# Chunk 1's second layer by seven products, with the sums for it spread over GpSimd and VectorE

## The chip, the core and the metric

The kernel runs on one core of a Trainium2 chip. The metric is the time of one execution in device microseconds. TensorE (PE, its weight loads PEld) multiplies into PSUM; VectorE (DVE), ScalarE (ACT) and GpSimd (POOL) work on what lies in SBUF or, GpSimd excepted here, in PSUM; SyncE (SP) and GpSimd issue the transfers. Each engine works off its own instructions strictly in the program's order.

## The reference

Strided sparse attention, and then a layer pair with a leaky kink between the layers. All inputs and the output are float32.

```python
# q, k, v: (8, 8, 576, 64); stride 32; heads 0-3 local, heads 4-7 strided
scores = np.matmul(q, k.transpose(0, 1, 3, 2)) / np.sqrt(64)
mask_local   = (rel >= 0) & (rel < 32)          # rel = query position - key position
mask_strided = (rel >= 0) & (key % 32 == query % 32)
attn = softmax(where(mask, scores, -1e9))
x = matmul(attn, v) -> (4608, 512)
h = x @ w_in                                    # (512, 2048)
g = np.maximum(h, 0.0) + alpha * np.minimum(h, 0.0)
out = g @ w_out                                 # (2048, 512)
```

## The kernel before

The 4608 tokens are nine chunks of 512. For a chunk the first layer makes gT, 2048 features by 512 tokens in fp16, in 16 pieces (`lin1_piece`: four matmuls of 512 columns into a PSUM bank, Relu of the negative by ScalarE, the sum by VectorE, which writes one sixteenth of gT). The second layer multiplies gT with w_out.

Between these pieces TensorE does the attention of the next batch. It is cut into steps that stand in one list, `pieces`, and `attn_step` takes the next one: S are the scores of a pair of heads (`score_both`: matmuls, exponentials by ScalarE, then a multiplication with the mask), P a product with v (`pv_piece`, with a reciprocal and a multiplication by VectorE), T a turn of q or k (`transpose_piece`), X a turn of the result into xT, which is what the first layer reads. Some results are turned by a transfer instead (`x_dma`, and `x_copy` by ScalarE after it). A pair g belongs to batch g // 4; its heads are local for g % 4 below 2, strided above. The second half of an S's exponentials and its mask are put off to the next steps (`defer`). The steps also issue casts and loads for later batches.

The main loop runs over the chunks n from 1 and over i: i below 16 are pieces of the first layer, i from 16 are parts of the second. After each, a share of the attention steps is dealt out by an accumulator (`acc`). Chunk 0 stands in a list written out by hand before that loop, with the second layer of chunk 0 (`U`, `W`) and the attention of batch 1.

There are two forms of the second layer. `lin2_piece`, which chunk 1 takes, has 16 parts of four matmuls of 512 columns. `lin2_fast`, which chunks 2 to 8 take, computes the same by seven products in place of eight: gT is split in halves by token and by even and odd features, w_out in halves by column and by even and odd features, and the products are made of sums and differences of the quarters. It has 14 parts of eight matmuls of 256 columns. It needs four tiles of differences of w_out (`wsum`, made once, by `wout_sum` during chunk 1's second layer, each one VectorE operation of 128 x 2048) and four tiles of sums of gT (`gsum`, made for every chunk, each in two halves of 128 x 1024 by `g_sum`; two of the eight halves go to GpSimd, six to VectorE). Its parts stand in the order of products 1, 5, 6, 2, 7, 3, 4, two parts each. Product 5 reads gsum0 and wsum0, product 6 gsum1 and wsum1, product 7 gsum2 and wsum2, product 3 gsum3, product 4 wsum3. Products 3 and 7 end in a store that adds a saved part by VectorE (L688).

The mask multiplications are at L396 (VectorE, for pairs of batch 1), L401 and L408 (GpSimd, for all later pairs). `hps` and `ops` banks come from a PSUM pool of three, the banks of S's second half, P, T and X from another pool of three ("ps").

Of the kernel before, what the change touches and what calls it, by code (L numbers as in the profile page):

```python
# [9 lines left out]
F32 = mybir.dt.float32  # L10
# [22 lines left out]
def kernel(  # L33
# [50 lines left out]
    DX = 2  # L84
# [271 lines left out]
    def score_both(P, eng=None):  # L356

        w, r = P.w, 72 if P.strided else 128
        for i in range(2):
            et = ets[ectr["i"] % NE]  # L360
            ectr["i"] += 1
# [26 lines left out]
            if eng is not None:  # L388
                if i == 0:
                    keep(nc.scalar.activation(  # L390
                        ev.rearrange("r (y c) -> r y c", y=2), sp[0:r, :, 0:n], AF.Exp, scale=SCALE))
# [4 lines left out]
                keep(nc.vector.tensor_tensor(mv, mv, m, op=ALU.mult))  # L396
                continue
            if i == 0:
                keep(nc.scalar.activation(  # L399
                    ev.rearrange("r (y c) -> r y c", y=2), sp[0:r, :, 0:n], AF.Exp, scale=SCALE))  # L400
                keep(nc.gpsimd.tensor_tensor(mv, mv, m, op=ALU.mult))  # L401
                continue

            def ex(y):
                keep(nc.scalar.activation(  # L405
                    ev[:, n * y : n * y + n], sps[y][0:r, 0:n], AF.Exp, scale=SCALE))
                if y:
                    keep(nc.gpsimd.tensor_tensor(mv, mv, m, op=ALU.mult))  # L408

            defer_et["et"] = et  # L410
            defer.extend([lambda: ex(0), lambda: ex(1)])
# [88 lines left out]
    for g in range(7, npair + 2):  # L500
# [30 lines left out]
        for i, (kind, fn) in enumerate(seq):  # L531
# [6 lines left out]
            def run(fn=fn, extra=extra, g=g, c=c, kind=kind, lastp=(i == lastP), first=(i == 0),  # L538
                    second=(i == min(1, len(seq) - 1))):
                fn()  # L540
                for b, pr in extra:
                    if pr in ("q", "k"):
                        if b < NX:
                            cast_l(b, pr)
                        if b + 1 < NX:
                            load_qk(b + 1, pr)
                        continue
                    cast_v(b, pr, "pool")
                    if pr == 1 and b + 1 < B:
                        load_v(b + 1, True)  # L550
# [4 lines left out]
                if lastp:  # L555
                    if 4 * DX <= g - 1 < npair and pairs[g - 1].xd:
                        x_dma(pairs[g - 1])
                    if g % 4 == 3 and DX < c + 1 < B:
                        transpose_d()
                    if g % 4 == 2 and DX <= c and c + 1 < B:  # L560
                        load_d(c + 1)
                    if g % 4 == 1 and DX <= c and c + 1 < B:
                        load_v(c + 1, False)
                    if g % 4 == 1 and NX <= c + 2 < B:
                        load_rows(c + 2, "q")
                    if g == 8:
                        load_v(3, True)
# [54 lines left out]

    ops_cur = {}

    def lin2_piece(n, i):
        mt, part = i // 4, i % 4
        last = n == NCH - 1
        if part == 0:
            ops_cur["t"] = phpool.tile([128, 512], F32, tag="hps", name="ops")
        ops = ops_cur["t"]  # L630
        r0 = 512 * n + 128 * mt
        if last and mt == 3:

            if part in (1, 3):
                return
            c0 = 128 * part
            half = phpool.tile([128, 512], F32, tag="hps", name="ops3") if part else ops
            for kf in range(16):
                keep(nc.tensor.matmul(
                    half[:, 0:256], gTs[n][:, kf, 128 * mt : 128 * mt + 128],  # L640
                    wout16[:, kf, c0 : c0 + 256], start=(kf == 0), stop=(kf == 15)))
            osb = opool.tile([128, 512], F32, tag="osb", name="osb")
            keep(nc.vector.tensor_copy(osb[:, 0:256], half[:, 0:256]))
            keep(nc.sync.dma_start(out[r0 : r0 + 128, c0 : c0 + 256], osb[:, 0:256]))
            return
        for kf in range(4 * part, 4 * part + 4):
            keep(nc.tensor.matmul(  # L647
                ops, gTs[n][:, kf, 128 * mt : 128 * mt + 128], wout16[:, kf, :],
                start=(kf == 0), stop=(kf == 15)))
        if part == 3:  # L650
            osb = opool.tile([128, 512], F32, tag="osb", name="osb")
            keep(nc.scalar.copy(osb, ops))
            keep(nc.sync.dma_start(out[r0 : r0 + 128, :], osb))


    def wout_sum(i):

        def w(j, c):
            return wout16.rearrange("p (i j) c -> p i j c", j=2)[:, :, j, 256 * c : 256 * c + 256]

        o, a, b = (
            (0, w(0, 1), w(0, 0)), (1, w(1, 1), wsum[0]),
            (2, w(1, 1), w(0, 1)), (3, w(1, 0), wsum[1]))[i]
        keep(nc.vector.tensor_tensor(wsum[o], a, b, op=ALU.subtract))

    def g_sum(n, i, h, eng="dve"):

# [260 lines left out]
                keep(nc.sync.dma_start(out[384:512, :], osb))  # L928
        return run

    def sc1(g):
        return lambda: score_both(pairs[g], "dve")

    for fn in [
        vs(1, 0, "pool"), sc1(6), U(0), vs(1, 1, "pool"), U(1), sc1(7), U(2), U(3), Cl(1, "q", "act"), Pv(6, 1),
        Cl(1, "k"), Pv(6, 2), Pv(6, 0), U(4), U(5), Pv(7, 0), Pv(7, 1), U(6), loads2, T(2, "q"), U(7), Pv(7, 2), W(0), W(1),
        T(2, "k"), U(8), X(7, "act"), U(9), W(2), sc1(4), W(3), ov(1, "dve", 0, 24), U(10), sc1(5), W(4), U(11),
        X(6, "act"), Pv(4, 1), W(5), Cl(2, "q", "act"), Cl(2, "k", "act"), U(12), Pv(5, 1), U(13), Pv(4, 0), U(14), Pv(5, 0),
        U(15), W(6), X(4, "dve"), X(5, "dve"), W(7)]:
        fn()  # L940
    for pr in range(2):
        cast_v(2, pr, "pool")
    wide["on"] = False
# [12 lines left out]
    for n in range(1, NCH):  # L956
        ab = attn_until(n + 1) if n + 1 < B else len(pieces)
        left = ab - pos["i"]
        acc = -1.5 if n == 1 else 0.0
        for i in range(32 if n < FAST else 30):  # L960
            if i < 16:
                lin1_piece(n, i if n < FAST else 8 * (i // 8) + 2 * (i % 4) + i % 8 // 4)
            elif n < FAST:
                lin2_piece(n, i - 16)
            else:
                lin2_fast(n, i - 16)
            acc += left / (22 if n < FAST else 19.5 if n == B - 2 else 21) * (0.5 if i < 16 else 1.0)
            cnt = int(acc)
            acc -= cnt
# [5 lines left out]
            for z, h, eng in (sums2 if n == FAST else sums).get(i, ()):  # L975
                g_sum(n, z, h, eng)
        while pos["i"] < ab:
            attn_step(ab)

# [29 lines left out]
```

## Time and profile before

| | us |
|---|---|
| median of three runs | 297.71 (297.05 to 299.68) |
| profiled execution, its own time | 297.54 |
| its span, first to last instruction | 295.7 |
| busy: PE, DVE, ACT, POOL | 290.9, 214.5, 179.9, 175.2 |
| granted TensorE clock | 1.00 throughout |

The difference between the execution's time and its span lies before the first and after the last instruction. Busy times of different engines overlap. A row of the timeline has the start, the duration, the engine, the line and the tiles; two instructions of one engine that follow each other closely can overlap by about 0.1 us, since one begins while the other drains, so the spacing of starts is what an instruction occupies of its engine's queue.

### The profile page before, as it was taken

Reading aid. Unit: us, or ns where it says so; the run is one execution under the profiler, and the core shown is the slowest. Engines: PE = TensorE matmul, PEld = TensorE weight load, DVE = VectorE, ACT = ScalarE, POOL = GpSimd, SP = SyncE. Lnnn points to the kernel's source line nnn. Section 1 sums busy time; section 2 is a strip of 40 time slices with the busy share of each in tenths; the row PEclk is TensorE's granted clock in tenths of the full one; section 3 lists DMA queues with packets and bytes.
Section 4 is the critical chain, followed back from the end, with each engine's and each line's share of the span. In section 5 each row is a group of like instructions: output and inputs, shape, how many; then the busy total and the mean of one; then the engine's idle time right before and its main releaser. Section 6 shows DMA issues by size and latency. Waiting matters only on the chain.

```text
span 295.7 us, 6837 instructions
## 1 busy us (share of the span) xinstructions
PE 290.9 (98%) x2684; PEld 183.1 (62%) x2684; DVE 214.5 (73%) x404; ACT 179.9 (61%) x334; POOL 175.2 (59%) x164
## 2 busy tenths in 40 slices
PE   8999999999999999999999999999999999999995
PEld 3764555544554478646864686468645964784584
DVE  5688875668675897588848984898489858926852
ACT  1677766797557774775477647764776257416630
POOL 8362535059989998979896987585463305002200
PEclk9999999999999999999999999999999999999999
DMA  7999999999999969999999999967611130022004
GB/s 182 260 191 202 233 214 252 214 166 317 135 223 151 117 99 99 194 174 127 162 204 131 138 158 212 135 92 115 170 22 21 49 117 2 0 73 71 0 2 142
DMA packets 96975, 41.17 MB, mean 139 GB/s; under 512 B 75360, under 2 KB 93232, under 8 KB 96944
## 3 DMA queue, kind: packets, MB, share of 16 engines
q0 software_dynamic: 51008, 17.77, 59.5%
q1 hardware_dynamic: 45584, 22.32, 37.6%
q10 hardware_dynamic: 352, 0.66, 0.9%
q8 instruction: 21, 0.34, 0.5%
q14 instruction: 10, 0.08, 0.1%
HBM read 38.24 MB, written 9.44 MB: 161 GB/s over the span
## 4 chain that ended last, share of the span: by engine, by line
PE 82%; DMA 13%; POOL 2%; DVE 1%; issue 1%; ACT 0%; DVEq 0%; ACTq 0%; POOLq 0%
PE hps L608 36%; PE ops L743 21%; PE ops L733 8%; DMA win<-in_moe_w_in_dram 7%; DMA wout<-in_moe_w_out_dram 6%; PE ops L647 5%; PE pv L429 4%; PE sp L376 2%; PE ops L908 2%; PE sph L376 1%; PE tp L292 1%; PE ops L923 1%; PE xp L454 1%; POOL win L778 1%; DVE gT L619 1%; POOL vl L222 1%
## 5 line engine op out<-in xcount | busy, mean ns | idle before, releaser
L608 PE MATMUL hps<-xT,win 128*128 128x512 f16 x576 | 132.4, 379 | 0.0
L619 DVE SCALAR_TENSOR_TENSOR gT<-neg,oma,hps 128x512 f16<-128x512 f32 x144 | 105.3, 744 | 36.3 <-ACT neg L616 28.5
L616 ACT ACTIVATE neg<-hps 128x512 f32<-128x512 f32 x144 | 85.8, 598 | 34.3 <-PE hps L608 32.2
L608 PEld LDWEIGHTS <-win 128*128 128x128 f16 x576 | 53.5, 98 | 58.2 <-issue 0.2
L677 POOL TENSOR_TENSOR gsum<-gT 128x1024 f16<-128x1024 f16 x14 | 29.7, 2122 | 41.7 <-DVE gT L619 36.7
L401 POOL TENSOR_TENSOR et<-et,consts 128x576 f16<-128x576 f16 (+1 forms) x24 | 33.8, 1409 | 24.2 <-ACT et L399 23.8
L743 PEld LDWEIGHTS <-gT 128*128 128x128 f16 x336 | 31.5, 98 | 5.4 <-issue 0.3
L438 DVE TENSOR_TENSOR x<-pv,rc 96x384 f16<-96x384 f32 (+2 forms) x62 | 33.0, 532 | 2.1
L408 POOL TENSOR_TENSOR et<-et,consts 128x576 f16<-128x576 f16 (+1 forms) x24 | 33.4, 1392 | 0.0
L429 PEld LDWEIGHTS <-et 72*128 72x128 f16 (+1 forms) x448 | 23.7, 98 | 9.7 <-ACT et L339 0.4
L743 PE MATMUL ops<-wout,gT 128*128 128x256 f16 x224 | 27.9, 272 | 0.1
L733 PE MATMUL ops<-wsum,gsum 128*128 128x256 f16 x216 | 26.5, 273 | 0.0
L399 ACT ACTIVATE et<-sp 128x576 f16<-128x576 f32 (+1 forms) x24 | 15.5, 644 | 17.1 <-PE sp L376 17.1
L234 POOL COPY vs<-stv 72x1024 f16<-72x1024 f16 x14 | 15.3, 1104 | 15.8 <-DMA stv<-in_v_dram 15.8
L436 DVE RECIPROCAL rc<-pv 72x6 f32<-72x6 f32 (+2 forms) x80 | 14.7, 184 | 11.2 <-PE pv L429 10.8
L743 PEld LDWEIGHTS <-gsum 128*128 128x128 f16 x224 | 20.9, 98 | 2.6
L733 PEld LDWEIGHTS <-gsum 128*128 128x128 f16 x224 | 20.7, 98 | 2.7
L688 DVE TENSOR_TENSOR osb<-ops,par 128x512 f32<-128x512 f32 (+1 forms) x14 | 9.4, 673 | 15.7 <-PE ops L743 8.2
L405 ACT ACTIVATE et<-sph 128x288 f16<-128x288 f32 (+1 forms) x48 | 18.8, 408 | 0.0
L686 ACT COPY osb<-ops 128x512 f32<-128x512 f32 x14 | 8.2, 587 | 16.4 <-PE ops L743 16.3
L647 PE MATMUL ops<-wout,gT 128*128 128x512 f16 x64 | 16.4, 379 | 0.0
L760 ACT COPY par<-ops 128x512 f32<-128x512 f32 x13 | 7.6, 586 | 12.8 <-PE ops L733 12.3
(110 smaller groups left out, 359.4 us busy)
## 6 DMA issues: line engine op xcount, KB each, us to landing
out_dram<-osb SPq DMA_DIRECT2D x35, 256.0 KB, 4.6
vl<-in_v_dram POOLq DMA_DIRECT2D x6, 384.0 KB, 9.2
win<-in_moe_w_in_dram POOLq DMA_DIRECT2D x4, 512.0 KB, 17.4
wout<-in_moe_w_out_dram POOLq DMA_DIRECT2D x4, 512.0 KB, 17.4
qsd<-in_q_dram POOLq DMA_DIRECT2D x7, 288.0 KB, 6.0
ksd<-in_k_dram POOLq DMA_DIRECT2D x7, 288.0 KB, 8.0
stv<-in_v_dram POOLq DMA_DIRECT2D x7, 288.0 KB, 7.4
ql<-in_q_dram SPq DMA_DIRECT2D x3, 576.0 KB, 9.1
```

Source lines behind the costliest of these rows:

```text
L401: keep(nc.gpsimd.tensor_tensor(mv, mv, m, op=ALU.mult))
L405: keep(nc.scalar.activation(ev[:, n * y : n * y + n], sps[y][0:r, 0:n], AF.Exp, scale=SCALE))
L408: keep(nc.gpsimd.tensor_tensor(mv, mv, m, op=ALU.mult))
L429: keep(nc.tensor.matmul(pv[:, 65 * x : 65 * x + 65], et[0:r, c : c + 128], v16[0:r, 2 * P.pr + hh, t, :] if P.strided else v16[:, 6 * (2 * ...
L438: keep(nc.vector.tensor_tensor(P.x16[0:w, c0 : c0 + 64 * nb].rearrange("r (c e) -> r c e", e=64), pvv[:, :, 0:64], rc[0:w, 0:nb].unsqueeze ...
L608: keep(nc.tensor.matmul(hps, win16[:, kk, 128 * m : 128 * m + 128], xT[:, kk, c0 : c0 + 512], start=(kk == 2), stop=(kk == 1)))
L616: keep(nc.scalar.activation(neg, hps, AF.Relu, scale=-1.0))
L619: keep(nc.vector.scalar_tensor_tensor(gTs[n][:, m, :], neg, oma[:, m : m + 1], hps, op0=ALU.mult, op1=ALU.add))
L647: keep(nc.tensor.matmul(ops, gTs[n][:, kf, 128 * mt : 128 * mt + 128], wout16[:, kf, :], start=(kf == 0), stop=(kf == 15)))
L677: keep((nc.vector if eng == "dve" else nc.gpsimd).tensor_tensor(gsum[i][:, hs], a, b, op=op))
L733: keep(nc.tensor.matmul(o, gsum[i][:, y, 128 * z : 128 * z + 128], wsum[i][:, y, :], start=(x == "5" and y == 0 and (z == 0 or alone)), st ...
L743: keep(nc.tensor.matmul(o, lhs(y), rhs(y), start=(first and y == 0), stop=(y == 7), skip_group_check=True))
```

## The change

Chunk 1 takes `lin2_fast` too, and `lin2_piece` goes. For that wsum0 to wsum2 must be there before chunk 1's second layer: GpSimd makes wsum0, wsum1 and half of wsum2 at the end of chunk 0, behind the loads for batch 2; VectorE makes the rest in chunk 1's second layer (i = 21 and 24). Chunk 1 makes its eight gsum halves by the table `early`, one by GpSimd (i = 11) and seven by VectorE. The attention steps of chunk 1 are dealt by a fixed rule: one after each even i from 2 to 14, one after each i from 16, and two after i = 24 and 25. Pair 11's two masks go from GpSimd to VectorE, pair 5's from VectorE to GpSimd, and pair 5's products come after pair 4's. The casts of batch 3's q and k go from GpSimd to ScalarE and, with the loads of batch 4's q and k, from attention steps at about i = 10 and 12 to i = 16. The load of batch 3's v goes from i = 12 to i = 17.

```diff
 def score_both(P, eng=None):
+        mul = (nc.vector if P.g == 11 else nc.gpsimd).tensor_tensor
...
-                keep(nc.vector.tensor_tensor(mv, mv, m, op=ALU.mult))
+                keep((nc.vector if eng == "dve" else nc.gpsimd).tensor_tensor(mv, mv, m, op=ALU.mult))
...
-                keep(nc.gpsimd.tensor_tensor(mv, mv, m, op=ALU.mult))
+                keep(mul(mv, mv, m, op=ALU.mult))
...
                     if pr in ("q", "k"):
+                        if b == 3:
+                            continue
...
-                    if g % 4 == 1 and DX <= c and c + 1 < B:
+                    if g % 4 == 1 and DX < c and c + 1 < B:
                         load_v(c + 1, False)
...
-    def wout_sum(i):
+    def wout_sum(i, eng="dve", h=None):
+        hs = slice(0, 8) if h is None else slice(4 * h, 4 * h + 4)
...
-        X(7, "act"), U(9), W(2), sc1(4), W(3), ov(1, "dve", 0, 24), U(10), sc1(5), W(4), U(11),
-        ..., U(12), Pv(5, 1), U(13), Pv(4, 0), U(14), Pv(5, 0),
+        X(7, "act"), U(9), W(2), sc1(4), W(3), ov(1, "dve", 0, 24), U(10), sc1(5, "pool"), W(4), U(11),
+        ..., U(12), Pv(4, 0), U(13), Pv(5, 0), U(14), Pv(5, 1),
         U(15), W(6), X(4, "dve"), X(5, "dve"), W(7)]:
         fn()
+    wout_sum(0, "pool")
+    wout_sum(1, "pool")
+    wout_sum(2, "pool", 0)
     for pr in range(2):
         cast_v(2, pr, "pool")
...
-    FAST = 2
+    early = {
+        11: [(0, 0, "pool")], 16: [(0, 1, "dve"), (1, 0, "dve")], 17: [(1, 1, "dve")],
+        19: [(2, 0, "dve")], 20: [(2, 1, "dve")], 22: [(3, 0, "dve"), (3, 1, "dve")]}
...
-        acc = -1.5 if n == 1 else 0.0
-        for i in range(32 if n < FAST else 30):
+        acc = 0.0
+        for i in range(30):
             if i < 16:
-                lin1_piece(n, i if n < FAST else 8 * (i // 8) + 2 * (i % 4) + i % 8 // 4)
-            elif n < FAST:
-                lin2_piece(n, i - 16)
+                lin1_piece(n, 8 * (i // 8) + 2 * (i % 4) + i % 8 // 4)
             else:
                 lin2_fast(n, i - 16)
...
+            if n == 1:
+                cnt = 1 + (i in (24, 25)) if i > 15 else int(i > 0 and i % 2 == 0)
+            else:
+                acc += left / (19.5 if n == B - 2 else 21) * (0.5 if i < 16 else 1.0)
+                ...
             attn_n(cnt, ab)
-            if n < FAST:
-                if i in (18, 21, 24, 27):
-                    wout_sum((i - 18) // 3)
-                continue
+            for z, h, eng in {1: early, 2: sums2}.get(n, sums).get(i, ()):
+                g_sum(n, z, h, eng)
+            if n > 1:
+                continue
+            if i == 16:
+                for nm in "qk":
+                    cast_l(3, nm, "act")
+                    load_qk(4, nm)
+            if i == 17:
+                load_v(3, False)
+            if i == 21:
+                wout_sum(2, "dve", 1)
+            if i == 24:
+                wout_sum(3)
```

More of the change, by code (lines that the diff above doesn't have):

```diff
@@ L623 @@
     ops_cur = {}
[L625 to L653, printed above, removed]
[L656 removed]
+    def wout_sum(i, eng="dve", h=None):
+        hs = slice(0, 8) if h is None else slice(4 * h, 4 * h + 4)
         def w(j, c):
[L659 removed]
+            return wout16.rearrange("p (i j) c -> p i j c", j=2)[:, hs, j, 256 * c : 256 * c + 256]
         o, a, b = (
[L662 to L664 removed]
+            (0, w(0, 1), w(0, 0)), (1, w(1, 1), wsum[0][:, hs]),
+            (2, w(1, 1), w(0, 1)), (3, w(1, 0), wsum[1][:, hs]))[i]
+        keep((nc.vector if eng == "dve" else nc.gpsimd).tensor_tensor(wsum[o][:, hs], a, b, op=ALU.subtract))
     def g_sum(n, i, h, eng="dve"):
@@ L929, in W, with sc1 @@
         return run
-    def sc1(g):
-        return lambda: score_both(pairs[g], "dve")
+    def sc1(g, eng="dve"):
+        return lambda: score_both(pairs[g], eng)
     for fn in [
```

13 lines of the change are left out of this document (5 added, 8 removed).

## The prediction

> **What bounds the kernel now.** I read the page first, then the chain that ended last.
>
> ```profile
> span 295.7 us, 6837 instructions
> PE 290.9 (98%) x2684; PEld 183.1 (62%) x2684; DVE 214.5 (73%) x404; ACT 179.9 (61%) x334; POOL 175.2 (59%) x164
> ```
>
> TensorE is busy for 98% of the span, so first of all a change is worth what it does to TensorE's own work, and whatever it does elsewhere counts only where it makes TensorE wait. The chain has the stretch in question, chunk 1's second layer from 72.43 on, with attention pieces between its parts, and chunk 2's second layer, which is already done by seven products:
>
> ```profile
> 72.43 0.86 PE ops L647 x4
> 73.48 0.86 PE ops L647 x4
> ...
> 75.39 0.24 PE sp L376 x8
> 75.75 0.97 PE ops L647 x4
> ...
> 77.77 0.50 PE tp L292 x9
> ...
> 105.98 0.87 PE ops L743 x8
> ```
>
> Four matmuls of 512 columns take 0.86 us, eight of 256 columns 0.87. Between them a P (six small products, 73.29 to 73.48) costs 0.19 us, a T (nine transposes) 0.50, an S (scores) 0.36 and 0.11 more in the part behind it. Then I set the two stretches beside each other in the busy times by stage (columns: length, then busy time of PE, PEld, DVE, ACT and POOL):
>
> ```profile
> 72.43:90.47 18.04, 18.04 (x181) 9.68 (x180) 12.54 (x24) 10.91 (x23) 16.97 (x14) 1.00 1.69 179
> 105.98:121.51 15.53, 15.53 (x196) 13.53 (x194) 11.50 (x24) 9.64 (x17) 14.46 (x14) 1.00 1.05 116
> ```
>
> TensorE has no gap in either, at granted clock 1.00. GpSimd is nearly full in chunk 1's stretch (16.97 of 18.04 us), VectorE has 5.5 us free. These two spare amounts are what the change spends.
>
> **What it takes from TensorE.** Chunk 1's second layer has 16 parts of four 512-column matmuls, 16 x 0.86 = 13.8 us. After, it has 14 parts of eight 256-column matmuls, 14 x 0.875 = 12.2 us. The 22 attention pieces between them stay, and their order does too. Through the first layer they fall where they fell (after the parts 2, 4, ... 14), so TensorE reaches 72.43 as before. Saved: **1.6 us**, if nothing waits. The weight loads double per column, but chunk 2's stretch above carries them (13.53 of 15.53) with no gap.
>
> **GpSimd's w_out differences.** They stand behind the loads for batch 2, where GpSimd waits for v:
>
> ```profile
> 62.62 2.02 POOL L234 COPY vs<-stv 72x1024 f16<-72x1024 f16 x2 [14.55 <-DMA stv<-in_v_dram]
> 49.16 0.65 ACT L390 ACTIVATE et<-sp 128x576 f16<-128x576 f32 x1 [0.29 <-PE sp L376]
> 53.45 0.35 PE L429 MATMUL pv<-vl,et 128*128 128x65 f16 x6
> 67.10 0.35 PE L429 MATMUL pv<-vl,et 128*128 128x65 f16 x6
> L677 POOL TENSOR_TENSOR gsum<-gT x14: 2111/2123/2137, 101.3 to 274.8; 128x1024 f16<-128x1024 f16 x14
> ```
>
> Pair 5's two masks come to GpSimd first: from 49.85 (when the exponential ends), about 1.25 us each, to 52.35. Its last product at 53.45 still finds both; the new order, pair 5 after pair 4, is what makes that so. Then two and a half differences of 2048 elements. The trace has no such operation on GpSimd. Its nearest row is the sum of 1024, 2.12 us and very even, so 4.2 each and **10.5 in all, to 62.8**. At half that time nothing changes, since v lands at 62.6; at 1.5 times it, GpSimd is 5.3 us late and pair 8's first mask, due at 64.65 plus 1.3 for a product that starts at 67.1, has only 1.1 us in hand, so that TensorE would stall by some 4 us. I take 10.5: VectorE does nothing with two SBUF inputs in those 10 us, so nothing holds it up. Cost: nothing, the cover being the 14.55 us wait.
>
> **GpSimd in chunk 1.** Before:
>
> ```profile
> 69.18 1.27 POOL L408 TENSOR_TENSOR et<-et,consts 128x576 f16<-128x576 f16 x1
> 70.39 1.14 POOL L234 CAST ql<-ql 128x1152 f16<-128x1152 f32 x1
> 72.58 1.52 POOL L222 DMA_DIRECT2D vl<-in_v_dram  x1
> 75.35 2.27 POOL L408 TENSOR_TENSOR et<-et,consts 72x576 f16<-72x576 f16 x1
> 75.26 1.23 DVE L664 TENSOR_TENSOR wsum<-wout 128x2048 f16<-128x2048 f16 x1
> ```
>
> The two casts (2.3 us) go to ScalarE, the v load is issued later, pair 11's two masks (1.3 and 2.3 before) go to VectorE, and one gsum half (2.1) comes. So GpSimd is relieved by about 4 us: that half runs 70.4 to 72.5, pair 10's masks 72.5 to 74.9, the q and k loads of batch 3 to 76.4 and the v load to 77.9. The half is read at 74.55, its own margin 2 us. ScalarE has 7.1 us free in the stretch (18.04 less 10.91) and takes 2.3 for the casts at about 73.3, for T pieces that read them at 77.8: hidden.
>
> **VectorE's queue is where it gets tight.** Prices:
>
> ```profile
> L677 DVE TENSOR_TENSOR gsum<-gT,gsum x14: 678/680/685, 112.4 to 284.7; 128x1024 f16<-128x1024 f16 x14
> L664 DVE TENSOR_TENSOR wsum<-wout,wsum x2: 1401/1442/1484, 80.1 to 86.7; 128x2048 f16<-128x2048 f16 x2
> L664 DVE TENSOR_TENSOR wsum<-wout x2: 1231/1320/1409, 75.3 to 82.3; 128x2048 f16<-128x2048 f16 x2
> L396 DVE TENSOR_TENSOR et<-et,consts 72x576 f16<-72x576 f16 x4 | 1.8, 452 | 0.6 <-ACT et L390 0.5
> L688 DVE TENSOR_TENSOR osb<-ops,par 128x512 f32<-128x512 f32 x13 | 9.0, 692 | 15.6 <-PE ops L743 8.2 <-issue 7.4
> ```
>
> Out go the four differences, 5.5 us. In come seven gsum halves (4.8), one and a half differences (2.1), two masks (0.9) and two adding stores (1.4): 9.2. That makes 12.54 + 3.7 = **16.2 us of work in a stretch of 16.4**. Chunk 2 has only 11.5 there. An average of 99% says that the order decides, so I walk the queue, with these spacings from start to start:
>
> ```profile
> 73.10 0.75 DVE L619 SCALAR_TENSOR_TENSOR gT<-neg,oma,hps 128x512 f16<-128x512 f32 x1 [0.41 <-ACT neg L616]
> 106.29 0.18 DVE L436 RECIPROCAL rc<-pv 72x6 f32<-72x6 f32 x1
> 106.98 0.73 DVE L619 SCALAR_TENSOR_TENSOR gT<-neg,oma,hps 128x512 f16<-128x512 f32 x1
> 112.37 1.28 DVE L677 TENSOR_TENSOR gsum<-gT,gsum 128x1024 f16<-128x1024 f16 x2
> 107.03 1.28 POOL L401 TENSOR_TENSOR et<-et,consts 72x576 f16<-72x576 f16 x1
> 107.75 1.12 DVE L677 TENSOR_TENSOR gsum<-gT 128x1024 f16<-128x1024 f16 x1
> ```
>
> A reciprocal and its product take 0.69 (106.29 to 106.98), 0.56 for the short form, a gsum half 0.64, a mask about 0.38. The last two rows show a collision: VectorE's sum took 1.12 instead of 0.68, ending 0.6 after GpSimd's mask ended at 108.31. So it began only when the mask was through.
>
> From 73.76: pair 9's product to 74.45. The half (0,1) now waits for GpSimd's mask until 74.9 and ends at 75.5; (1,0) 76.15; product 76.85; (1,1) 77.5; mask 77.9; product 78.6; mask 79.0; (2,0) and (2,1) 80.3; pair 10's second product 81.0; half difference 81.7; (3,0), (3,1) 82.95; its third product 83.5; pair 11's first 84.2; last difference 85.6; second product 86.3, third 86.85.
>
> TensorE meets these in its own order, 0.875 a part and the pieces as above (all 15 together 18.04 less 13.8, so 4.2 us). Product 5 wants (0,1) at 75.8 (there at 75.5); product 6 wants gsum1 at 76.9 and 78.2 (76.15, 77.5); product 7 wants (2,1) and the half difference at 81.65 and 82.1 (80.3, 81.7). All just in time. The small PSUM pool of three buffers is what binds: pair 10's first P takes the one that pair 9's last product frees at 76.85, 0.2 late. Pair 11's first P, now directly behind an S and the 24th part, wants the one freed at 83.5 some 0.4 before. The next S wants the one freed at 86.3, 0.45 before. Sum of **stalls 1.05 us**.
>
> The Trainium skill, page "SBUF — State Buffer", section "Who interferes with whom", has that wait as a lock: an operation of VectorE with two SBUF inputs and one of GpSimd that reads SBUF exclude each other for a whole instruction. The trace agrees (1.12 against 0.68 us). By it the 0.45 at 74.9 is due in full; with the two engines merely sharing, the walk above would come out some 0.4 us better.
>
> **Then xT for chunk 2.** Its first layer needs pair 10's turned x and pair 11's:
>
> ```profile
> 81.93 0.42 DVE L438 TENSOR_TENSOR x16s<-pv,rc 72x256 f16<-72x256 f32 x1
> 82.77 1.27 SPq L468 DMA_TRANSPOSE xs<-x16s  x1
> xs<-x16s SPq DMA_TRANSPOSE x1, 4.9
> 88.43 1.41 ACT L477 COPY xT<-xs 128x384 f16<-128x384 f16 x2
> 89.72 0.72 ACT L230 COPY xT<-xp 128x384 f16<-128x384 f16 x2
> ```
>
> Before, the product ended at 82.35, the turn landed at 87.7, and the copies ended at 90.4, just ahead of 90.47. After, the product is later (83.5), the turn lands at 88.5, its copies end at 89.8, pair 11's at 90.15; TensorE, with its 1.05 us of stalls, is there at 89.65 and wants pair 11's rows at 89.87. Another 0.3 us. Chunk 2 then starts as if at 90.0: **0.5 us saved of 1.6**. The bounds: no stall at all, 1.6; every queue as walked, 0.5. The walk puts every term on its late side where two were near (the S at 0.47, a mask that may come sooner). I take **0.8**.
>
> Against its own execution: 297.54 us with a span of 295.7; span after 294.9, time 296.7. The median of the three runs is 297.71, 0.17 above that execution, so I forecast **296.9 us**.
>
> **The rivals.** *All of the 1.6 us arrives* (296.1): the stalls above hang on margins of 0.2 to 0.45 us, and ScalarE and VectorE could be 0.4 us ahead of my walk throughout. Against it: 16.2 us of VectorE work in 16.4. Chance 0.20.
>
> *The gain is given back in full* (297.7): VectorE's collisions are repeated, say at the halves (1,0) and (3,0) as well, 0.45 each; then the S and pair 11's copies end near 91. For it: chunk 2 shows both 1.12 and a second slow sum. Against: GpSimd only issues loads from 74.9 to about 77.9, and waits for pair 12's exponential until about 83. Chance 0.20.
>
> *Slower: the moved loads hold up the turns.* Batch 4's q and k were issued at 65.5 and 67.0 and now go out at about 74, on SyncE's queue, ahead of pair 9's turns and pair 10's:
>
> ```profile
> 65.54 1.41 SPq L104 DMA_DIRECT2D ql<-in_q_dram  x1
> ql<-in_q_dram SPq DMA_DIRECT2D x1, 576.0 KB, 9.1
> vl<-in_v_dram POOLq DMA_DIRECT2D x1, 384.0 KB, 8.9
> DMA  7999999999999969999999999967611130022004
> ```
>
> In the 40 slices DMA stands at 9 here throughout. Two loads of 576 KB, with the v load behind them, run until 84 to 87. If the turn of pair 10, issued at 83.6, needs 7.4 us instead of 4.9, it lands at 91.0, its copies end at 92.3, pair 11's at 92.65 against 90.4 before; TensorE is by then at least 1.3 us later than before after all: 299.0. It decides from a landing of about 89 on, each further microsecond being one of the time. Against it: those loads are due by 83, and 70 to 74 loses the same bytes. Chance 0.15, a third of it beyond 300.7.
>
> *That seven products cost as much as eight* is ruled out by the chain's rows (0.87 against 0.86 for a part, 14 against 16).
>
> **How the numbers follow.** Forecast 0.45 (its own range 296.4 to 297.4), full gain 0.20, nothing 0.20, slower 0.15. The low end takes the full gain less the 0.5 that a median of these runs may be off: 295.6. The high end is the slow rival's price, 299.0; what it leaves out is its tail. A measurement of this kernel tells about 1%, 3 us, from no change. A gain over 1% would need twice what TensorE can save: 0.02. Slower by more than that: the tail of the last rival, 0.05. Within: 0.93.
>
> **What would show it.** Second-layer matmuls of chunk 1 should be 112 of 256 columns, with none of L647's kind; GpSimd's differences at 2.1 to 4.3 us between 52 and 63, and pair 8's first mask still at about 64.7. Chunk 1's second layer should take 16.4 to 17.6 us with VectorE near 16 us busy in it. Short gaps of TensorE ahead of pair 11's first P and pair 13's S, and ahead of chunk 2's second K slice, would show the walk right. It is wrong if GpSimd's differences run past 64, if P waits for v, if the turn lands later than 89, or if later chunks' stretches (15.5 us for chunk 2's second layer) grow.

## The result, and the profile after

The changed kernel is slower: 302.31 us (299.34 to 304.23, six runs) against 297.48 us (297.05 to 299.68, six runs) of the kernel before on the same chip, a ratio of 1.0127 [1.0091, 1.0163]. Ratios here are formed from the single runs without those marked as slow, in this case the slowest of the six, so they differ a little from those of the medians. The forecast was 296.9 us with a range of 295.6 to 299.0. It was wrong, in sign and in size.

The profiled execution took 304.23 us, with a span of 302.4 against 295.7. It is that slowest run, so its waits are the loss at its largest. The busy times by stage (columns as in the prediction: length, then PE, PEld, DVE, ACT, POOL, then the granted clock) put the whole difference in one place. The rows are chunk 1's second layer, chunk 2's first layer and its second:

```profile
72.52:97.26 24.74, 18.66 (x229) 15.31 (x228) 15.05 (x33) 13.62 (x26) 18.49 (x16) 0.86 1.78 168
97.26:112.77 15.51, 15.51 (x123) 7.49 (x121) 12.24 (x21) 11.45 (x22) 12.21 (x12) 1.00 1.16 126
112.77:128.19 15.42, 15.42 (x196) 13.54 (x194) 10.77 (x24) 9.65 (x17) 11.36 (x12) 1.00 0.88 131
```

TensorE reaches the second layer at 72.52 (before 72.43) and needs 24.74 us for it, where the kernel before needed 18.04. Chunk 2 is as before. What TensorE waited for in that stretch (what it waited for, us in total, times, the longest), and the matmuls around those waits:

```profile
PE pv L430 <- DMA vl<-in_v_dram: 5.1, 1, 5.1
PE sph L377 <- DVE x L439: 0.9, 1, 0.9
```

```profile
86.92 0.30 PE L377 MATMUL sph<-qT,kT 64*128 64x96 f16 x5 [0.88 <-DVE x L439]
87.16 1.05 PE L717 MATMUL ops<-wout,gsum 128*128 128x256 f16 x8
93.31 0.49 PE L430 MATMUL pv<-vl,et 128*128 128x65 f16 x6 [5.11 <-DMA vl<-in_v_dram]
93.61 1.90 PE L717 MATMUL ops<-wsum,gT 128*128 128x256 f16 x8
```

P of pair 12, the first product of batch 3, waits 5.11 us for v. The last row is the third loss: the part after the wait takes 1.90 us instead of 1.04. The same busy times cut finer, at the wait and behind it:

```profile
87.00:93.30 6.30, 1.20 (x13) 0.80 (x14) 1.10 (x2) 0.71 (x2) 6.28 (x7) 0.73 2.07 131
93.30:97.26 3.96, 3.95 (x31) 3.12 (x32) 0.74 (x2) 2.10 (x4) 3.96 (x4) 0.57 1.26 238
```

The granted clock was 0.57 in the 3.96 us behind the wait, which at full speed are 0.57 x 3.96 = 2.26 us: 1.7 lost. So 24.74 = 18.04 + 5.1 + 0.9 + 1.7 - 1.0, and the 1.0 is what is left of the saving of 1.6 by these idle times. The Trainium skill, page "TensorE: Matmul & The Clock Gate", section "HAM oscillation — how this bites in real kernels", warns of idle gaps of TensorE longer than about 3.4 us, after which it starts at a lower clock. The trace agrees: 0.57 behind a gap of 5.11 us. Not every run has this loss: the mean clock was 1.00 in three of the six, one of them at 303.25 us.

The transfers themselves, each by its issue (start and duration of issuing) and its time from issue to landing. v, then the turn of pair 10's products, and the copy into xT that waits for that turn:

```profile
76.36 1.46 POOL L222 DMA_DIRECT2D vl<-in_v_dram  x1
vl<-in_v_dram POOLq DMA_DIRECT2D x1, 384.0 KB, 16.8
```

```profile
83.28 1.29 SPq L469 DMA_TRANSPOSE xs<-x16s  x1
xs<-x16s SPq DMA_TRANSPOSE x1, 10.1
93.37 1.40 ACT L478 COPY xT<-xs 128x384 f16<-128x384 f16 x2 [5.38 <-DMA xs<-x16s]
```

v was issued 3.8 us later than before (72.58) and took 16.8 us in place of 8.9, so it landed 11.7 us later. The turn took 10.1 us in place of 4.9. Its copies end at 94.8, under cover of the wait for v alone: with v in time, chunk 2's first layer would by these rows have waited for them. Both are late by the same cause, if there is one, and the experiments begin with it.

### The profile page after: what moved, and what is told of

It is laid out like the page before. It is cut to its first block, busy times and chain, and to the rows that moved or that the text cites. A ratio compares the mean times of both kernels' runs of the same rounds, so it can differ in the third digit from the quotient of the medians.

```text
span 302.4 us, 6943 instructions
## 1 busy us (share of the span) xinstructions
PE 290.7 (96%) x2732; PEld 188.4 (62%) x2732; DVE 214.7 (71%) x411; ACT 182.6 (60%) x337; POOL 183.4 (61%) x166
## 4 chain that ended last, share of the span: by engine, by line
PE 71%; DMA 18%; POOL 5%; ACT 2%; issue 2%; DVE 1%; DVEq 0%; ACTq 0%; POOLq 0%
PE hps L611 31%; PE ops L717 21%; PE ops L707 8%; DMA win<-in_moe_w_in_dram 7%; DMA wout<-in_moe_w_out_dram 6%; DMA vl<-in_v_dram 6%; PE pv L430 3%; PE ops L882 2%; PE sp L377 2%; ACT neg L619 2%; POOL et L409 1%; PE xp L455 1%; PE ops L897 1%; PE sph L377 1%; POOL et L402 1%
## 5 line engine op out<-in xcount | busy, mean ns | idle before, releaser
L651 POOL TENSOR_TENSOR gsum<-gT 128x1024 f16<-128x1024 f16 x15 | 31.8, 2122 | 41.7 <-DVE gT L622 36.7
L402 POOL TENSOR_TENSOR et<-et,consts 128x576 f16<-128x576 f16 (+1 forms) x23 | 33.8, 1471 | 35.6 <-ACT et L400 35.3
L717 PEld LDWEIGHTS <-gT 128*128 128x128 f16 x384 | 36.5, 99 | 6.6 <-issue 0.3
L717 PE MATMUL ops<-wout,gT 128*128 128x256 f16 x256 | 32.1, 272 | 0.1
L707 PE MATMUL ops<-wsum,gsum 128*128 128x256 f16 x248 | 30.7, 273 | 0.0
L409 POOL TENSOR_TENSOR et<-et,consts 128x576 f16<-128x576 f16 (+1 forms) x23 | 29.7, 1289 | 0.0
L717 PEld LDWEIGHTS <-gsum 128*128 128x128 f16 x256 | 23.7, 98 | 2.9
L707 PEld LDWEIGHTS <-gsum 128*128 128x128 f16 x256 | 23.7, 98 | 2.9
L662 DVE TENSOR_TENSOR osb<-ops,par 128x512 f32<-128x512 f32 (+1 forms) x16 | 10.8, 674 | 16.5 <-PE ops L717 9.1
L660 ACT COPY osb<-ops 128x512 f32<-128x512 f32 x16 | 9.4, 586 | 17.0 <-PE ops L717 16.9
L717 PE MATMUL ops<-wsum,gT 128*128 128x256 f16 x128 | 17.4, 286 | 0.0
L430 PE MATMUL pv<-vl,et 128*128 128x65 f16 x192 | 11.3, 195 | 5.1 <-DMA vl<-in_v_dram 5.1
```

What stands on the lines that cost most here:

```text
L402: keep(mul(mv, mv, m, op=ALU.mult))
L409: keep(mul(mv, mv, m, op=ALU.mult))
L430: keep(nc.tensor.matmul(pv[:, 65 * x : 65 * x + 65], et[0:r, c : c + 128], v16[0:r, 2 * P.pr + hh, t, :] if P.strided else v16[:, 6 * (2 * ...
L651: keep((nc.vector if eng == "dve" else nc.gpsimd).tensor_tensor(gsum[i][:, hs], a, b, op=op))
L707: keep(nc.tensor.matmul(o, gsum[i][:, y, 128 * z : 128 * z + 128], wsum[i][:, y, :], start=(x == "5" and y == 0 and (z == 0 or alone)), st ...
L717: keep(nc.tensor.matmul(o, lhs(y), rhs(y), start=(first and y == 0), stop=(y == 7), skip_group_check=True))
```

## The experiments

The theories were: A, the load of v, issued later and behind the other loads, is what costs; B, the loads of batch 4's q and k, moved into the same microseconds, slow everything that is under way there; C, VectorE's fuller queue costs, and the transfers only show it. Each is compared with the kernel before on the same chip, which took 297.35 to 297.64 us there. Waits, rows and times to landing are always those of the one profiled execution of a kernel.

### The two moved loads, one at a time

The changed kernel with v's load back where it was (q and k still late):

```diff
-                    if g % 4 == 1 and DX < c and c + 1 < B:
+                    if g % 4 == 1 and DX <= c and c + 1 < B:
...
-            if i == 17:
-                load_v(3, False)
```

> The changed kernel with the load of batch 3's v back at its old attention step (i = 12); all else as changed. Theory A (the v load stands too late in GpSimd's queue, behind q and k of batch 3): v lands by 83, TensorE's 5.1 us wait ahead of pair 12's first P goes, time 296.5 to 297.5. Theory B (the loads of batch 4's q and k, moved to i = 16, hold up everything behind them): v is there, but the turn of pair 10 still takes about 10 us and lands at about 93, so that chunk 2's first layer waits for xT; time 299.5 to 301. Theory C (VectorE's full queue is the cause): no better than 301.

The changed kernel with the loads of q and k back (v still late):

```diff
                         if b == 3:
+                            load_qk(4, pr)
                             continue
...
                     cast_l(3, nm, "act")
-                    load_qk(4, nm)
```

> The changed kernel with the loads of batch 4's q and k back at their old attention steps (i = 10 and 12), the casts of batch 3 still on ScalarE at i = 16, the v load still at i = 17. Theory A: v still lands at 89 or later, TensorE waits 2 to 5 us, time 299.5 or more. Theory B: v lands by 86 and the turn of pair 10 takes 5 to 6 us, no wait over 1 us, time 296.5 to 297.5. Theory C: no better than 301.

Both edits together:

> The changed kernel with both the v load of batch 3 and the loads of batch 4's q and k back at their old steps. Theories A and B: 296.3 to 297.3, what is left of the saving being 0.5 to 1.6 us less a collision of VectorE's first sum with GpSimd's masks, which come 1.5 us later by the v load. Theory C: no better than 301.

And the kernel before with nothing changed but these loads, which are put where the change puts them:

```diff
-                        if b + 1 < NX:
+                        if b + 1 < NX and b != 3:
...
-                    if g % 4 == 1 and DX <= c and c + 1 < B:
+                    if g % 4 == 1 and DX < c and c + 1 < B:
...
+            if n == 1 and i == 16:
+                for nm in "qk":
+                    load_qk(4, nm)
+            if n == 1 and i == 17:
+                load_v(3, False)
```

> The kernel before with nothing changed but the transfers: batch 4's q and k issued after i = 16 and batch 3's v after i = 17. Theories A and B: a wait of TensorE for v ahead of pair 12's first P and a late turn of pair 10, 3 to 6 us, time 300 to 304. Theory C: within 1 us of the kernel before, 297 to 298.5.

| kernel | q, k late | v late | us (median, range) | ratio to before | v, us to landing | pair 10's turn |
|---|---|---|---|---|---|---|
| before | no | no | 297.35 (297.25 to 297.90) | | 8.9 | 4.9 |
| before, loads moved | yes | yes | 304.60 (302.15 to 306.33) | 1.0233 [1.0168, 1.0299] | 16.7 | 8.8 |
| changed | yes | yes | 302.31 (299.34 to 304.23) | 1.0127 [1.0091, 1.0163] | 16.8 | 10.1 |
| changed, v early | yes | no | 300.96 (299.13 to 301.68) | 1.0108 [1.0069, 1.0147] | 10.4 | 7.1 |
| changed, q and k early | no | yes | 300.75 (299.44 to 301.86) | 1.0108 [1.0075, 1.0142] | 12.5 | 8.0 |
| changed, both early | no | no | 299.29 (299.25 to 300.11) | 1.0070 [1.0051, 1.0090] | 9.1 | 2.7 |

The kernel before, which knows nothing of seven products or of the new sums in chunk 1, loses 7.2 us to the moved loads alone. TensorE's wait in it, and the issue of v:

```profile
PE pv L429 <- DMA vl<-in_v_dram: 6.0, 1, 6.0
```

```profile
77.81 1.46 POOL L222 DMA_DIRECT2D vl<-in_v_dram  x1
```

So the moved loads are enough for a loss of this size, and C is not needed for it. A and B are both true in part: either load alone moved back leaves 3.4 to 3.6 us of loss, both moved back 1.9. The times to landing say how they work together: v takes 12.5 us when it alone is late, 16.8 when q and k go out with it. With either load back TensorE no longer waits for v at all; that it would, when v alone is late, was expected and did not come. It waits for xT instead (1.5 us with v early, 1.4 with q and k early) and for VectorE (2.3 and 2.8 us, in several waits).

Moved back together the loads bring 3.0 us of the 4.8 by the medians, and 1.7 of 3.8 by the ratios. All three theories missed the 299.29 us: A and B had expected 296.3 to 297.3, C no less than 301.

What is left in the kernel with both early shows in TensorE's waits, and in VectorE's and GpSimd's rows:

```profile
PE pv L430 <- DVE x L439: 1.2, 1, 1.2
PE sph L377 <- DVE x L439: 0.9, 1, 0.9
```

```profile
74.82 1.00 DVE L652 TENSOR_TENSOR gsum<-gT 128x1024 f16<-128x1024 f16 x1
75.74 1.76 DVE L652 TENSOR_TENSOR gsum<-gsum,gT 128x1024 f16<-128x1024 f16 x1
73.97 1.29 POOL L402 TENSOR_TENSOR et<-et,consts 72x576 f16<-72x576 f16 x1
75.21 1.73 POOL L409 TENSOR_TENSOR et<-et,consts 72x576 f16<-72x576 f16 x1
```

With v's load issued ahead of them, GpSimd's masks come 1.5 us later than in the changed kernel and meet VectorE's second sum as well as its first: 1.00 and 1.76 us in place of 0.68. So the later load of v had a use: it kept these two apart. By stage, chunk 1's second layer and chunk 2's:

```profile
72.80:91.77 18.97, 16.89 (x229) 14.36 (x228) 16.05 (x33) 13.49 (x26) 11.90 (x10) 1.00 1.35 189
107.30:123.20 15.90, 15.58 (x195) 13.58 (x194) 12.17 (x24) 9.67 (x17) 15.85 (x14) 1.00 0.98 117
```

TensorE works 16.89 us in the first and waits 2.1: 0.9 more than the 18.04 before, with its 1.15 us of saving inside. The second is 0.4 longer than before, with GpSimd at 15.85 of 15.90 us, and it was 0.4 late at 72.8 already: 1.7 in all, which is the difference of the spans (297.4 against 295.7). So most of this rest is C's, as waits for VectorE.

### The collision and the late difference

With both loads early, the first sum goes from GpSimd (i = 11) to VectorE (i = 10), to end GpSimd's part earlier:

```diff
-        11: [(0, 0, "pool")], 16: [(0, 1, "dve"), (1, 0, "dve")], 17: [(1, 1, "dve")],
+        10: [(0, 0, "dve")], 16: [(0, 1, "dve"), (1, 0, "dve")], 17: [(1, 1, "dve")],
```

> All transfers at their old steps (as in the kernel with both loads early, 299.3 us), and GpSimd's gsum half of chunk 1 made by VectorE after i = 10 instead, while it has room. GpSimd's masks of pair 10 then end at about 75.1 instead of 76.9. Theory D (what is left of the loss with the loads back is VectorE's sums waiting for GpSimd's masks, 1.2 us of TensorE ahead of pair 10's first P): that wait falls to 0.2 or less, time 298.0 to 298.4. Rival (the wait ahead of pair 13's S takes over what is saved, since VectorE's queue is full anyway): that wait grows from 0.9 to about 2, time 299.0 to 299.5.

299.37 us (298.97 to 300.19), ratio 1.0059 [1.0042, 1.0076]: no gain over both early (299.29, on another chip; the intervals overlap). VectorE, GpSimd, and what TensorE then waited for:

```profile
69.12 2.66 DVE L652 TENSOR_TENSOR gsum<-gT 128x1024 f16<-128x1024 f16 x1
68.72 1.28 POOL L402 TENSOR_TENSOR et<-et,consts 128x576 f16<-128x576 f16 x1
69.95 1.27 POOL L409 TENSOR_TENSOR et<-et,consts 128x576 f16<-128x576 f16 x1
72.49 1.02 PE L612 MATMUL hps<-xT,win 128*128 128x512 f16 x4 [2.44 <-DVE gT L623]
```

The sum started at 69.12, under GpSimd's mask, and ended when the second mask did, at 71.2 plus its own 0.6. The 1.2 us wait was not removed, it moved to another pair of masks and doubled: the first layer's banks were then freed 2.44 us late. The Trainium skill, page "SBUF — State Buffer", section "Who interferes with whom", says that such an operation, with two inputs from SBUF, contends with one of GpSimd that reads SBUF, and that contention there is an exclusive lock. The trace agrees, and goes further: the wait outlasts GpSimd's instruction when its next one stands right behind.

On top of that, the last difference of w_out a part earlier, ahead of pair 11's products in VectorE's queue no more:

```diff
-            if i == 24:
+            if i == 23:
                 wout_sum(3)
```

> The same with VectorE's last w_out difference one place earlier, after i = 23 instead of 24, where VectorE stood idle for 0.6 us. Theory (the wait ahead of pair 13's S is the length of VectorE's queue behind that difference): the wait falls from 0.9 to 0.3, time 0.6 below the kernel with the gsum half moved, 297.4 to 297.8. Rival (pair 11's first P is then late instead): no change, within 0.2 of it.

298.78 us (297.85 to 302.01), ratio 1.0044 [1.0012, 1.0076]. TensorE's wait for pair 13's S:

```profile
PE sph L377 <- DVE x L439: 0.2, 1, 0.2
```

The stall of 0.9 fell to 0.2 as expected, and the median by the 0.6 that this is worth, though the two intervals overlap. The time itself had been expected at 297.4 to 297.8, on top of a gain from the edit before that did not come.

### Room for v in chunk 1

Can v's load stay late if it goes out ahead of the strided q and k of batch 3? From the kernel with q and k early:

```diff
-            if i == 17:
+            if i == 16:
                 load_v(3, False)
```

> The changed kernel with batch 4's q and k loads at their old steps and the load of batch 3's v one place earlier, after i = 16, so that GpSimd issues it ahead of batch 3's strided q and k instead of behind them; it is issued at about 75, still 2 us later than before. Theory A' (v is late because it queues behind those two loads): v lands in 8 to 10 us, by 85, the turn of pair 10 in 3 to 6 us, no wait of TensorE beyond the 0.9 ahead of pair 13's S, time 296.8 to 297.5. Rival (v is late because it is issued after 75 at all, into transfers that are then full): v lands at 88 or later, time 299 to 301.

300.07 us (298.77 to 302.23), ratio 1.0082 [1.0052, 1.0113]. TensorE's longest waits from chunk 1's second layer on, and the three loads:

```profile
PE hps L612 <- ACT xT L478: 1.2, 1, 1.2
PE sph L377 <- DVE x L439: 0.9, 1, 0.9
```

```profile
vl<-in_v_dram POOLq DMA_DIRECT2D x1, 384.0 KB, 10.2
qsd<-in_q_dram POOLq DMA_DIRECT2D x1, 288.0 KB, 13.0
ksd<-in_k_dram POOLq DMA_DIRECT2D x1, 288.0 KB, 12.7
```

P no longer waits for v. What v won, the strided loads lost (7.6 and 7.2 us with the order reversed), and the turns with them (pair 10's took 7.3 us), so that the copies into xT became the wait. This execution, at 301.67 us slower than the median, also waited for w_out (1.6 us) and for batch 2's turned k (1.2 us), both before v's load goes out, so that the edit has no part in them. The same with the last difference at i = 23:

> The same with VectorE's last w_out difference after i = 23 instead of 24. If v is there in time: 0.6 us below the one before, 296.2 to 296.9, and below the kernel before. If v is late: the same as the one before, within 0.3.

300.75 us (299.80 to 303.64), ratio 1.0106 [1.0046, 1.0166]. Pair 13's stall fell to 0.2 again, but the wait for xT was 2.3 us in this profile, the slowest of the four runs. Neither place of v in this stretch is enough, so the next kernel takes v out of it.

### Out of the stretch

So v's load goes to 60.7 us, behind GpSimd's differences, and VectorE's share of the differences leaves chunk 1: VectorE makes the first halves of all four at about 46 us, GpSimd the second halves in the stretch where it waits. The loads of q and k are at their old places, and the table of sums is that of the change:

```diff
+    def ws():
+        for z in range(4):
+            wout_sum(z, "dve", 0)
...
-        T(2, "k"), U(8), X(7, "act"), U(9), W(2), ...
+        T(2, "k"), ws, U(8), X(7, "act"), U(9), W(2), ...
...
-    wout_sum(0, "pool")
-    wout_sum(1, "pool")
-    wout_sum(2, "pool", 0)
+    for z in range(4):
+        wout_sum(z, "pool", 1)
+    load_v(3, False)
```

> Chunk 1 still by seven products. The first half of each w_out difference by VectorE at about 46 us, where it stands idle for 2.6 us and GpSimd only issues transfers; the second halves by GpSimd in its idle stretch (8.4 us instead of 10.3), and none in chunk 1. Batch 3's v is issued right behind them, at about 61 us; batch 4's q and k at their old steps. Theory (the seven products do save TensorE 1.2 to 1.6 us, and the change lost it by three things: late transfers, VectorE's full queue, collisions of VectorE's sums with GpSimd's masks): no wait over 0.5 us in chunk 1, time 296.0 to 296.8, below the kernel before. Rival (transfers have no room anywhere before 90 us, so that v, wherever it goes, holds up a turn): a wait for the turned q and k of batch 2 at about 71 or for xT at 90, time 298 or more.

298.54 us (296.83 to 301.91, twelve runs), ratio 1.0024 [0.9999, 1.0050]. That misses the 296.0 to 296.8 expected. Chunk 1's second layer took 17.99 us, and the profile lists no wait for VectorE or for a transfer in it on TensorE. But ScalarE, whose casts were to be hidden, waits for k of batch 3 and stands in TensorE's way for 0.8 us. With v's load ahead of it that k took 10.1 us to land, against 7.4 in the changed kernel and 7.5 in the one with both loads early: what v gained, k paid. ScalarE's wait, and TensorE's behind it:

```profile
76.02 1.15 ACT L230 CAST kl<-kl 128x1152 f16<-128x1152 f32 x1 [1.48 <-DMA kl<-in_k_dram]
```

```profile
PE ops L708 <- ACT ops L732: 0.5, 1, 0.5
PE tp L292 <- ACT et L406: 0.3, 1, 0.3
```

The same kernel with the loads of q and k at i = 16, as the change has them, asks whether these loads alone, without v, fit:

```diff
                         if b == 3:
-                            load_qk(4, pr)
                             continue
...
+                    load_qk(4, nm)
```

> The same with batch 4's q and k loaded after i = 16, where the change has them. Theory B alone (these 1.2 MB ahead of the turns of pairs 9 and 10 on SyncE's queue cost time by themselves): the turn of pair 10 lands at 89 or later, 0.8 to 2 us more than the kernel with them early, 297 to 298.5. Rival (with v gone by then there is room): within 0.4 of it.

298.33 us (297.33 to 299.88), ratio 1.0030 [1.0010, 1.0051], the same within the intervals. The turn took 5.2 us in place of 2.6 and there is half a microsecond of waiting for xT, no more. So the late q and k cost nothing that shows once v has left the stretch, which fits that in the changed kernel they did harm together with v.

Back to the kernel with q and k at their old places: there the cast of k is put two parts later:

```diff
-            if i == 16:
-                for nm in "qk":
-                    cast_l(3, nm, "act")
+            if i in (16, 18):
+                cast_l(3, "qk"[i // 18], "act")
```

> The kernel with the differences spread and v at 61 us (298.5 us), and batch 3's k cast by ScalarE after i = 18 instead of 16. In the profile of that kernel ScalarE stood 1.48 us for k to land, with the copy of product 1's bank and the exponentials of pair 11 behind it, and TensorE's chunk 1 lost about 1.3 us to that. Theory (that wait is what hides the saving now): ScalarE does not wait, chunk 1's second layer takes 16.7 to 17.1 us instead of 17.99, time 297.0 to 297.6. Rival (GpSimd, full in chunk 2's first layer, takes it back there): chunk 2's two stretches grow from 31.5 to over 32 us, time 298 or more.

297.51 us (296.79 to 302.60), ratio 0.9996 [0.9981, 1.0010]. By stage, chunk 1's second layer, then chunk 2's two:

```profile
72.29:89.49 17.20, 17.06 (x229) 14.43 (x228) 13.61 (x31) 13.58 (x26) 9.19 (x10) 1.00 1.05 201
89.49:104.97 15.48, 15.48 (x122) 7.44 (x120) 12.05 (x21) 11.48 (x23) 15.46 (x15) 1.00 1.50 146
104.97:120.97 16.00, 15.80 (x196) 13.50 (x195) 12.12 (x24) 9.65 (x17) 14.96 (x14) 1.00 1.06 129
```

With no long wait left, chunk 1's second layer takes 17.2 us against 18.04. But chunk 2's takes 16.0 against 15.53. GpSimd's queue is full ahead of it (15.46 of 15.48 us), as it was in the kernel before (15.49 of 15.51); TensorE now comes 0.8 us earlier, GpSimd's masks only 0.4, and they cover more of VectorE's first sum, which takes 1.56 us in place of 1.12:

```profile
106.93 1.56 DVE L652 TENSOR_TENSOR gsum<-gT 128x1024 f16<-128x1024 f16 x1
106.65 1.28 POOL L402 TENSOR_TENSOR et<-et,consts 72x576 f16<-72x576 f16 x1
107.89 1.73 POOL L409 TENSOR_TENSOR et<-et,consts 72x576 f16<-72x576 f16 x1
```

Two attempts at that, each from this kernel. The first takes GpSimd's casts of v out of chunk 2 and puts them into chunk 1, where GpSimd is idle:

```diff
-                    cast_v(b, pr, "pool")
+                    if b != 3:
+                        cast_v(b, pr, "pool")
...
+            if i == 17:
+                for pr in range(2):
+                    cast_v(3, pr, "pool")
```

> The same with GpSimd's two casts of batch 3's v (2 us) moved from the attention steps of pair 11's products to i = 17, into the 8.8 us in which GpSimd waits for pair 12's exponential. Rival theory of the run before (GpSimd's full queue in chunk 2 takes the saving back): GpSimd is 2 us ahead in chunk 2, whose second layer falls from 15.9 to 15.5 us, time 0.3 to 0.8 below the run before, 296.3 to 297.2. If GpSimd's queue in chunk 2 costs nothing: within 0.2 of the run before.

300.17 us (298.78 to 300.47), ratio 1.0074 [1.0051, 1.0097]. The time of 296.3 to 297.2 that was expected is missed by 3 us. Chunk 2's second layer did fall to 15.42 us, as expected, which fits that GpSimd's queue had held it up, though TensorE also comes 3 us later here; but in chunk 1 GpSimd's idle time was time in which VectorE did its sums:

```profile
77.75 2.02 POOL L234 COPY vs<-stv 72x1024 f16<-72x1024 f16 x2
78.10 2.23 DVE L653 TENSOR_TENSOR gsum<-gsum,gT 128x1024 f16<-128x1024 f16 x1
81.44 0.40 PE L292 MATMUL tp<-consts,ql 128*128 128x128 f16 x4 [1.62 <-DVE x16s L439]
```

The second gives one half of gsum2 in chunk 2 to VectorE, so that GpSimd's masks end sooner:

```diff
-        5: [(2, 0, "pool")], 9: [(0, 0, "pool")], 15: [(0, 1, "dve")],
-        17: [(1, 0, "dve"), (1, 1, "dve")], 19: [(2, 1, "dve")], 20: [(3, 0, "dve"), (3, 1, "dve")]}
+        9: [(0, 0, "pool")], 15: [(0, 1, "dve")],
+        17: [(1, 0, "dve"), (1, 1, "dve")], 19: [(2, 0, "dve"), (2, 1, "dve")], 20: [(3, 0, "dve"), (3, 1, "dve")]}
```

> The kernel with k cast later (297.5 us, level with the kernel before) with one more edit: in chunk 2 the gsum half that GpSimd makes after i = 5 is made by VectorE after i = 19. Theory (what is still lost lies in chunk 2's full GpSimd queue): GpSimd's masks of pair 15 end by 108 instead of 109.6, VectorE's sum there takes 0.7 to 1.0 us instead of 1.6, chunk 2 takes 31.0 to 31.2 us instead of 31.5, time 0.3 to 0.5 lower, 297.0 to 297.2. Rival (VectorE's extra sum costs as much, or the loss lies elsewhere): chunk 2 at 31.4 or more, time 297.4 or more.

296.76 us (296.12 to 300.81, twelve runs) against 297.50 (296.93 to 298.64, seventeen), ratio 0.9972 [0.9959, 0.9986]. VectorE's sum now starts behind the masks and takes its own time, and chunk 2's second layer is back at 15.42 us:

```profile
108.03 0.69 DVE L652 TENSOR_TENSOR gsum<-gT 128x1024 f16<-128x1024 f16 x1
106.54 1.28 POOL L409 TENSOR_TENSOR et<-et,consts 72x576 f16<-72x576 f16 x1
```

This version is faster than both kernels, by 0.7 us (0.3%) than the one before, less than half of the 1.6 that the matmuls promised. Its profiled execution, at 297.7 us, is not among its faster ones; it still has 0.9 us of waiting for batch 2's turned k and 0.2 for xT.

## Why the prediction was wrong

**The step that failed is the cost of the moved loads, which the sum behind 296.9 us puts at nothing and only the third rival, "the moved loads hold up the turns", follows.** There the mechanism was in the text, but with a chance of 0.15, and its price had two faults. First, that the loads "run until 84 to 87" goes by their old times to landing, 8.9 us for v, and a DMA row that was full already was set against the rival ("70 to 74 loses the same bytes"). With both loads moved, the same 384 KB took 16.8 us. Secondly, the rival followed only the turn, into xT. That P waits for v stood under what would make the prediction wrong and had no price, though the margin was there to be worked out: issued at 76.4, v had to land within some 11 us to be there for P, which the walk had in the last parts of the stretch, two parts ahead of 89.65. The kernel before with the loads moved shows this term alone at 7.2 us, the lower clock behind the wait included.

**The turn** was allowed 7.4 us at the worst and took 10.1. The rule of the text, that each microsecond beyond a landing of about 89 is one of the time, would have given 94.8 less 89.8, 5 us, almost the price of the wait for v; the two overlap in time.

**The clock** was nowhere in the sum: 1.7 us behind the long wait, in the profiled execution.

**TensorE's saving** of 1.6 us was sized right; what failed is its condition, "if nothing waits". The kernel with k cast later took 17.20 us against 18.04, a gain of 0.84, and the profile lists next to no wait in it. But short waits hide in the busy time, since the profile models the ends of matmuls. From start to start they show:

```profile
75.74 1.05 PE L708 MATMUL ops<-wsum,gsum 128*128 128x256 f16 x8
76.86 0.34 PE L430 MATMUL pv<-vs,et 72*128 72x65 f16 x6
77.91 0.91 PE L292 MATMUL tp<-consts,ql 128*128 128x128 f16 x9
78.66 1.04 PE L708 MATMUL ops<-wsum,gsum 128*128 128x256 f16 x8
```

The part ahead of pair 10's first P takes 1.12 us in place of 0.87 (before: 75.69 to 76.56), the turn of q 0.75 in place of 0.50 (before: 77.61 to 78.11), and pair 13's S 0.56 in place of 0.36. These are 0.7 us of the 0.8 that is missing.

**The walk of VectorE's queue** held within about half a microsecond throughout: the sum (0,1) ended at 75.5 as walked, with 0.97 us beside a mask; the last difference started at 84.4 and ended at 85.6, as walked. The 16.2 us of work were too many: VectorE was busy for 15.05 us of the whole longer stretch.

```profile
74.54 0.97 DVE L651 TENSOR_TENSOR gsum<-gT 128x1024 f16<-128x1024 f16 x1
```

The stall before pair 13's S was 0.88 (0.45 walked), that before pair 10's first P about 0.3 from start to start (0.2 walked), that before pair 11's first P was absent (0.4 walked): 1.05 in sum walked, about 1.2 found. One step behind the walk does not add up: 90.47 less 1.6 plus 1.05 is 89.92, where the prediction has TensorE at 89.65; with 89.92 its extra 0.3 us for xT falls away, and the 0.5 us saved comes out all the same. What the walk did not see is how near the collisions stood: they come when a mask is 1.5 us later, as in the kernel with both loads early.

**GpSimd's differences** were right: 4.2, 4.2 and 2.1 us forecast, to 62.8, with pair 8's first mask at 64.65.

```profile
52.44 4.06 POOL L638 TENSOR_TENSOR wsum<-wout 128x2048 f16<-128x2048 f16 x1
56.58 4.07 POOL L638 TENSOR_TENSOR wsum<-wout,wsum 128x2048 f16<-128x2048 f16 x1
60.60 2.13 POOL L638 TENSOR_TENSOR wsum<-wout 128x1024 f16<-128x1024 f16 x1
```

**The casts on ScalarE** were hidden here, as forecast, at 73.3 and 74.4; that they hang on k's landing showed only when v's load was put ahead of k's.

What stays open is by which way the other loads held v up. The runs show that its time to landing grows with what goes out beside it, and that another order on its own queue helps v (12.5 to 10.2 us) at the cost of the strided q and k (7.6 and 7.2 to 13.0 and 12.7); whether the queue or the DMA engines themselves were the limit was not separated.

## What to carry to other kernels

A transfer that is moved has no fixed duration to carry along: price it by the work that waits for it, with the margin from its new issue to that first use, and let the duration range up to twice what it was; here a factor of 1.9 decided the case. Putting loads later to keep an engine's queue free in one stretch cost time even for one of the two loads (1.5 to 1.7 us by the medians), and more for both, while q and k alone cost nothing that shows once v had left the stretch; of what was tried, issuing one much earlier helped, reordering did not. And when VectorE and GpSimd both have sums from SBUF, plan them by the clock time of both: idle time of the one is only free if the other has none of them then, and time that is won in one chunk can be given back in the next if a queue there is full.

## What the runs showed of the hardware that was not expected

In the six kernels of the table the same load of 384 KB took 8.9, 9.1, 10.4, 12.5, 16.7 and 16.8 us to landing by when it and the other loads were issued, and pair 10's turn by transfer took 2.6 to 10.1 us over all kernels. VectorE's sum of 128 x 1024, 0.68 us alone, took 2.66 us behind two masks of GpSimd that stood end to end. A wait of 5.11 us cost TensorE another 1.7 us by a granted clock of 0.57 in the 3.96 us behind it, whereas the stretch with a wait of 2.44 us kept a clock of 1.00:

```profile
66.00:80.00 14.00, 11.48 (x126) 7.18 (x124) 12.75 (x21) 9.97 (x20) 10.61 (x10) 1.00 1.30 248
```
